# A spectral filter and a mixture of experts: experts' rows gathered without drains, three of them behind scatters, and a filter tile with its halves swapped

## The chip, the cores and the metric

The kernel runs on one core of one Trainium2 chip. The time is the device time of one execution in microseconds (us). A core has five engines, each with an instruction order of its own: PE (matrix products; its weight loads are shown as PEld), DVE (VectorE), ACT (ScalarE), POOL (GpSimd) and SP (SyncE, which issues transfers here). ACT and POOL issue transfers too. A transfer stands in the order of the engine that issues it, and an instruction that waits holds up all that stands behind it on that engine.

## The reference

Eight sequences of 2496 tokens with 256 channels are filtered in the frequency domain. The filtered tokens go to one of 8 experts each; an expert keeps the 80 tokens with the highest gate weight, and all other rows of the output are zero.

```python
X = np.fft.rfft(x, axis=1)                       # x: (8, 2496, 256)
y = np.fft.irfft(X * (filt_r + 1j * filt_i), n=2496, axis=1).reshape(19968, 256)
logits = y @ w_gate                              # 8 experts
expert_idx = np.argmax(logits, axis=1)
gate_w = softmax(logits)[arange, expert_idx]
for e in range(8):
    tok = the (at most) 80 tokens of expert e with the highest gate_w
    out[tok] = gate_w[tok, None] * (np.maximum(y[tok] @ w1[e], 0) @ w2[e])
```

`w1[e]` is 256 x 1024 and `w2[e]` 1024 x 256, all in float32.

## The kernel before

**Filtering.** The transform is done as matrix products with tables. `x` comes in chunks (`load_x`, tiles `x`), three for each of the 8 sequences. `stage1` multiplies a chunk with the table `wf_t`, `turn_t` transposes, `stage2` multiplies with the table `d_t` (tile `pb`), and `filtered` multiplies with the filter `ft` on DVE and adds on POOL (`yt`). The filter is brought into the order of `ft` at the start: `filter_in` loads five pieces (groups of four frequency rows) of `filt_r` from SP's queue and of `filt_i` from POOL's into the tile `fst`, whose partitions hold the real rows at places 0 and 1 of each four and the imaginary ones at 2 and 3; `filter_turn` multiplies `fst` with the permutation table `perm` into `pf`. On SP, each piece is followed by a piece of `d_t`, and behind the five pieces the x chunks 3 to 6. Ahead of the first piece stands a one-element copy on POOL from x chunk 1 into `fst[0, 0, 0]`. The tile framework sees that the loads into the real rows overwrite that element and lets them wait for the copy; so SP's filter loads, and all that stands behind them on SP, start when x chunk 1 has arrived. POOL's loads of the imaginary rows stand behind the copy in POOL's order.

**Gates and choice.** The filtered spectrum gives the gates directly (`gates`, `logits`, `gating`), and DVE finds the chosen tokens: `gating(3, 8)` turns the keys of the last two sequences on PE (`pk`), ACT copies them (`kt`), DVE takes the best eight of each row, `threshold` spreads them (`spread`), PE sums them up (`pall`), and DVE finds the threshold.

**Rows of the chosen tokens.** Only chosen tokens are transformed back. `gather_rows` fetches rows of a table with an indirect transfer on POOL (`gt`), `turn_rows` transposes them on DVE (`wt`), and `fill(n)` issues the next n of 20 products per tile that add up the tokens' rows (`pr`) from spectra kept in DRAM (`page`). There are seven such tiles; at the end of each, ACT copies it (`yr`) and writes it to `y_sel` in DRAM from its own queue. `fill` calls are set by hand between other work, and this fixes PE's order.

**Experts.** `experts(..., True)` runs the 8 experts. The rows of experts 0 and 1 are fetched ahead (`xg_first`) without the last tile, which a product adds. For experts 2 to 7, `gather(e)` fetches 80 rows of `y_sel` into a buffer `xg` on POOL, each followed by `nc.gpsimd.drain()`, by which POOL waits for what it has issued. In the loop, `layer1(e + 1)` (tile `ph`), `back(e - 1)` (tile `pb`, then `put`) and `layer2(e)` (tile `po`, with the turn `px` of the rows of expert e + 2 in its middle) follow each other on PE. `put` scales the result on ACT into one of two buffers `ys` and scatters it to the output with an indirect transfer on POOL. Each scatter writes the whole output tensor as far as the framework can see, so each waits for the one before to land; and `ys` of expert e waits for the scatter of expert e - 2. In POOL's order all six gathers stand ahead of the first scatter.

**Weights.** An expert's weights are one tile of two halves, `w1[e]` and `w2[e]`, loaded from SP (1 MB each, about). Tiles are reused, so a load waits for the last reader of the tile's former content. A `mark` is a one-element POOL memset into the tile ahead of the load: the load waits for it, and so for POOL to come to that place. `load_weights(3, ...)` is marked behind the gathers of experts 0 and 1, `load(4, ...)` behind the gather of expert 3. `load(5)` to `load(7)` follow in the loop.

`experts(..., False)` belongs to a branch for inputs that the fast path cannot hold; it is not taken here.

## Time and profile before

| what | value |
|---|---|
| three runs | 392.21, 395.75, 397.69 us; median 395.75 |
| the profiled execution, its own time | 397.52 us |
| its span, from the first to the last instruction | 395.7 us |
| mean granted PE clock | 0.969 |

The page gives, for each engine, busy time, share of the span and instructions; then the span in 40 slices of 9.9 us. A digit is a busy share in tenths; PEclk is the granted clock of PE in tenths of full speed.

```profile
PE 361.6 (91%) x4037; PEld 321.6 (81%) x4037; DVE 235.8 (60%) x509; ACT 131.1 (33%) x273; POOL 177.6 (45%) x256
...
PE   8789999999999999999999998999998998790793
...
POOL 3664355545646454444468887135534011201221
PEclk9999999999999999999999999999999999877597
...
GB/s 213 233 333 256 160 336 265 305 332 308 338 303 291 349 311 309 347 295 304 353 278 303 243 252 272 404 378 410 409 410 352 228 240 22 288 368 232 27 28 24
```

PE is busy in nearly every slice but the first and the last six. Those last slices hold the experts, from about 322 us on; there the clock drops as well. The transfers that the change touches are these (line, what goes where, issuing queue, count, size of each):

```profile
w<-in_moe_w_dram SPq DMA_DIRECT2D x16, 1024.0 KB
x<-in_x_dram SPq DMA_DIRECT2D x15, 936.0 KB
x<-in_x_dram SPq DMA_DIRECT2D x7, 702.0 KB
fst<-in_filt_i_dram POOLq DMA_DIRECT2D x10, 128.0 KB
fst<-in_filt_r_dram SPq DMA_DIRECT2D x10, 128.0 KB
```

### The profile page before, as it was taken

To read this page: it belongs to the slowest core of one execution; us is meant where nothing else is said; L and a number is where in the kernel's file an instruction comes from. 1 tells how busy PE (TensorE), PEld (TensorE's weight loads), DVE (VectorE), ACT (ScalarE), POOL (GpSimd) and SP (SyncE) were. 2 spreads that over 40 slices of the span, in tenths; PEclk is the share of its full clock that TensorE was granted. 3 is DMA by queue.
4 is the path that set the end of the run, shared out by engine and by line. 5 is a ranking of instruction groups with operands and counts; after the bars stand their busy time and mean duration, and the time that the engine had idled before them with its cause. 6 is when DMAs were issued, how large, how long until landed. Compare 5 with 4: busy or idle time off the path is not lost. (4 is left out here: it accounts for less than half of the span.)

```text
span 395.7 us, 9875 instructions
## 1 busy us (share of the span) xinstructions
PE 361.6 (91%) x4037; PEld 321.6 (81%) x4037; DVE 235.8 (60%) x509; ACT 131.1 (33%) x273; POOL 177.6 (45%) x256
## 2 busy tenths in 40 slices
PE   8789999999999999999999998999998998790793
PEld 7789989989899899799699896788864677690682
DVE  5037466748868668789797678899678311110010
ACT  2444545454455354444344452250000001000110
POOL 3664355545646454444468887135534011201221
PEclk9999999999999999999999999999999999877597
DMA  6798699999999999999988787999999670896000
GB/s 213 233 333 256 160 336 265 305 332 308 338 303 291 349 311 309 347 295 304 353 278 303 243 252 272 404 378 410 409 410 352 228 240 22 288 368 232 27 28 24
DMA packets 40975, 109.87 MB, mean 278 GB/s; under 512 B 3975, under 2 KB 14085, under 8 KB 39167
## 3 DMA queue, kind: packets, MB, share of 16 engines
q1 hardware_dynamic: 36008, 97.64, 72.8%
q0 software_dynamic: 3632, 10.46, 7.7%
q10 hardware_dynamic: 1282, 1.06, 0.8%
q8 instruction: 34, 0.56, 0.6%
q14 instruction: 19, 0.16, 0.1%
HBM read 70.35 MB, written 40.37 MB: 280 GB/s over the span
## 5 line engine op out<-in xcount | busy, mean ns | idle before, releaser
L356 POOL TENSOR_TENSOR yt<-p 128x256 f32<-128x256 f32 x159 | 114.9, 746 | 93.1 <-DVE p L348 90.3
L348 DVE TENSOR_TENSOR p<-pb,ft 128x1024 f32<-128x1024 f32 x80 | 97.3, 1217 | 55.7 <-PE pb L338 22.2
L313 PE MATMUL pa<-wf_t,x 117*128 117x120 f32 x704 | 92.0, 278 | 2.8 <-DMA x<-in_x_dram 2.8
L313 PEld LDWEIGHTS pa<-wf_t,x 117*128 117x128 f32 x704 | 86.2, 195 | 3.4 <-issue 2.9
L338 PE MATMUL pb<-d_t,t 128*128 128x128 f32 x640 | 84.9, 276 | 1.3 <-DVE p L348 1.2
L338 PEld LDWEIGHTS pb<-d_t,t 128*128 128x128 f32 x640 | 77.8, 192 | 2.0 <-ACT zt_last L422 1.2
L318 ACT COPY tt<-pa 128x480 f32<-128x480 f32 x96 | 47.9, 516 | 71.8 <-PE pa L313 70.7
L331 ACT COPY t<-pt 128x512 f32<-128x512 f32 x80 | 47.0, 588 | 18.4 <-PE pt L327 15.1
L369 DVE STREAM_TRANSPOSE u<-yt 128x512 f32<-128x512 f32 x70 | 48.9, 699 | 0.0
L327 PE MATMUL pt<-ident,tt 128*128 128x128 f32 x320 | 48.5, 274 | 0.5 <-ACT tt L318 0.5
L875 POOL DMA_INDIRECT gt<-rows_tbl,idxr x28 | 28.5, 1019 | 37.8 <-DVE wt L885 31.1
L327 PEld LDWEIGHTS pt<-ident,tt 128*128 128x128 f32 x320 | 37.4, 142 | 1.8 <-issue 1.6
L894 PE MATMUL pr<-page,wt 128*128 128x256 f32 x160 | 36.6, 382 | 0.1
L894 PEld LDWEIGHTS pr<-page,wt 128*128 128x128 f32 x160 | 29.6, 190 | 4.5 <-issue 0.9
L899 PE MATMUL pr<-page,wt 128*32 128x256 f32 x480 | 28.7, 380 | 1.1 <-issue 0.8
L885 DVE STREAM_TRANSPOSE wt<-gt 128x640 f32<-128x640 f32 x28 | 22.8, 830 | 7.3 <-DMA gt<-rows_tbl,idxr 7.0
L899 PEld LDWEIGHTS pr<-page,wt 128*32 128x32 f32 x480 | 15.6, 110 | 12.7 <-issue 2.0
L1215 DVE COPY xs_True<-px_True 128x160 f32<-128x160 f32 x8 | 2.6, 325 | 36.5 <-PE px_True L1212 24.7
L1196 POOL DMA_INDIRECT xg_True<-y_sel,idxg x6 | 5.7, 946 | 35.7 <-issue 35.7
L1245 PE MATMUL po_True<-hT_True,w 128*64 128x80 f32 x448 | 21.5, 258 | 0.0
L903 ACT COPY yr<-pr 128x256 f32<-128x256 f32 x7 | 2.6, 372 | 57.1 <-PE pr L894 27.0
L1227 PE MATMUL ph_True<-xs_True,w 128*64 128x80 f32 x512 | 20.9, 245 | 0.0
(215 smaller groups left out, 327.9 us busy)
## 6 DMA issues: line engine op xcount, KB each, us to landing
out_dram<-zero_t SPq DMA_DIRECT2D x32, 624.0 KB
yf<-u SPq DMA_DIRECT2D x56, 320.0 KB
page<-yf SPq DMA_DIRECT2D x14, 1280.0 KB
w<-in_moe_w_dram SPq DMA_DIRECT2D x16, 1024.0 KB
x<-in_x_dram SPq DMA_DIRECT2D x15, 936.0 KB
x<-in_x_dram SPq DMA_DIRECT2D x7, 702.0 KB
fst<-in_filt_i_dram POOLq DMA_DIRECT2D x10, 128.0 KB
fst<-in_filt_r_dram SPq DMA_DIRECT2D x10, 128.0 KB
```

Of the source, the lines that this page charges most:

```text
L313: nc.tensor.matmul(out=ps[:, j, :], rhs=wf_t, start=True, stop=True, lhsT=xt[3 * b + ch][:, j0 + j - JC * ch, 128 * cb:128 * cb + 128])
L318: nc.scalar.copy(out=tt[h][:, :, H3 * j0:H3 * j0 + hn * jn].rearrange("p s (j h) -> p s j h", h=hn), in_=v)
L327: nc.tensor.transpose(ps[:, i, :], tt[h][:, 2 * s:2 * s + 2, :].rearrange("p r n -> p (r n)"), ident[:])
L331: nc.scalar.copy(out=t2[k][:], in_=ps[:])
L338: nc.tensor.matmul(out=ps[:, :, i, :], lhsT=t[:, i, :], rhs=d_t[:, SG * g + i, :], start=True, stop=True)
L348: nc.vector.tensor_tensor(out=p[:], in1=f.unsqueeze(2).to_broadcast(shape), op=AL.mult, in0=ps[:].rearrange("p r s q -> p r (s q)").unsque ...
L356: eng.tensor_tensor(out=y[:, :, 2 * r:2 * r + 2, :], in0=a, in1=b, op=op)
L369: nc.vector.transpose(uu[h][:, :, SG * g:SG * g + SG, :].rearrange("p a s w -> p s a w"), spectrum(h)[:, SG * g:SG * g + SG])
L875: nc.gpsimd.indirect_dma_start(out=gts[t, g][:].rearrange("p s q -> p (s q)"), out_offset=None, in_=quarters, in_offset=bass.IndirectOffse ...
L885: nc.vector.transpose(wts[t][:, :, 32 * g:32 * g + 32], gts.pop((t, g))[:])
L894: nc.tensor.matmul(st["po"][:], lhsT=wts[t][:, s, :], rhs=columns(pages[t], s), **kw)
L899: nc.tensor.matmul(st["po"][at], lhsT=wts[t][:, s, at], rhs=columns(pages[source(t, g)[0]], s), **kw)
```

## The change

It has four parts.

1. The imaginary filter goes to places 0 and 1 of each four partitions of `fst` and the real one to 2 and 3; the table `perm` is swapped in the same way, so `ft` holds what it held. The one-element copy now touches the imaginary rows, which POOL loads; SP's loads of the real rows do not wait for it.
2. The four fills that stood behind `gating(3, 8)` stand ahead of it.
3. A drain is put on POOL behind the gathers of table rows for the last tile (`gather_all(6)`).
4. Experts: the gathers of 2, 3 and 4 stand in a row without drains. The gathers of 5, 6 and 7 move into the loop, each behind the scatter of expert 0, 1 and 2; one drain stands behind the last. The weights of expert 3 are loaded in two parts: `w1` where both were, `w2` with a mark of its own behind the gather of expert 3. The mark of expert 4's weights moves behind the gather of expert 4. There are four `xg` buffers instead of six, and three `ys` buffers instead of two.

```diff
-            perm.transpose(2, 0, 1, 3, 4).reshape(128, 2 * (NQ + NS - 1)).astype(f32))
+            perm[::-1].transpose(2, 0, 1, 3, 4).reshape(128, 2 * (NQ + NS - 1)).astype(f32))
...
-                        out=fst[2 * v + part:128:4, SG * g:SG * g + SG, :],
+                        out=fst[2 * (1 - v) + part:128:4, SG * g:SG * g + SG, :],
...
-        def load_weights(e, mark=None):
+        def load_first(e, mark=None):
             where, tag = WT[e]
             ws[e] = where.tile([128, NDB * FF + NFC * C], F32, name=f"w_{e}", tag=tag)
             if mark is not None:
                 mark(ws[e][:, 0:1], 0.0)
             nc.sync.dma_start(out=ws[e][:, 0:NDB * FF].rearrange("p (k f) -> p k f", k=NDB),
                               in_=moe_w1[e].rearrange("(k p) f -> p k f", p=128))
+
+        def load_second(e, mark=None):
+            if mark is not None:
+                mark(ws[e][:, NDB * FF:NDB * FF + 1], 0.0)
             nc.sync.dma_start(out=ws[e][:, NDB * FF:].rearrange("p (k d) -> p k d", k=NFC),
                               in_=moe_w2[e].rearrange("(k p) d -> p k d", p=128))
+
+        def load_weights(e, mark=None):
+            load_first(e, mark)
+            load_second(e)
...
-        fill(9)
+        fill(13)
         gating(3, 8)
-        fill(4)
...
         gather_all(6)
+        nc.gpsimd.drain()
...
-        load_weights(3, nc.gpsimd.memset)
+        load_first(3, nc.gpsimd.memset)
...
-            xg = fp.tile([cap, C], F32, name=f"xg_{first}_{e}", tag="xg", bufs=E - near)
+            xg = fp.tile([cap, C], F32, name=f"xg_{first}_{e}", tag="xg",
+                         bufs=4 if first else E)
...
-            ys = fp.tile([cap, C], F32, name=f"ys_{first}_{e}", tag="ys")
+            ys = fp.tile([cap, C], F32, name=f"ys_{first}_{e}", tag="ys", bufs=3)
...
-        for e in range(near, E):
+        for e in range(near, 5 if first else E):
             gather(e)
-            if first:
-                nc.gpsimd.drain()
             if first and e == 3:
+                load_second(3, nc.gpsimd.memset)
+            elif first and e == 4:
                 load(4, nc.gpsimd.memset)
...
             if e > 0:
                 back(e - 1)
+            if first and 0 < e < 4:
+                gather(e + 4)
+                if e == 3:
+                    nc.gpsimd.drain()
             layer2(e, (lambda: turn(e + 2)) if e + 2 < E else None)
```

POOL's order in the expert stage, before (drains are not listed; `w_3786` is the weight tile of expert 3, `w_3897` that of expert 4; `xg` are the gathers, `out_dram` the scatters):

```order
L1081 MEMSET w_3786 128x1
L1196 DMA xg_True_3887<-y_sel,idxg 80x256
L1196 DMA xg_True_3892<-y_sel,idxg 80x256
L1081 MEMSET w_3897 128x1
L1196 DMA xg_True_3901<-y_sel,idxg 80x256
L1196 DMA xg_True_3906<-y_sel,idxg 80x256
L1196 DMA xg_True_3911<-y_sel,idxg 80x256
L1196 DMA xg_True_3916<-y_sel,idxg 80x256
L1271 DMA out_dram<-ys_True_4092,idxs 19968x256
L1271 DMA out_dram<-ys_True_4180,idxs 19968x256
L1271 DMA out_dram<-ys_True_4268,idxs 19968x256
```

And the same stretch of POOL after the change (`w_3787` is expert 3's tile, `w_3901` expert 4's):

```order
L1081 MEMSET w_3787 128x1
L1205 DMA xg_True_3887<-y_sel,idxg 80x256
L1205 DMA xg_True_3891<-y_sel,idxg 80x256
L1087 MEMSET w_3787 128x1
L1205 DMA xg_True_3897<-y_sel,idxg 80x256
L1081 MEMSET w_3901 128x1
L1280 DMA out_dram<-ys_True_4076,idxs 19968x256
L1205 DMA xg_True_4081<-y_sel,idxg 80x256
L1280 DMA out_dram<-ys_True_4168,idxs 19968x256
L1205 DMA xg_True_4173<-y_sel,idxg 80x256
L1280 DMA out_dram<-ys_True_4260,idxs 19968x256
L1205 DMA xg_True_4265<-y_sel,idxg 80x256
```

The first scatter has moved ahead of the last three gathers, expert 4's mark behind one gather more, and a second mark of expert 3's tile stands between the gathers of experts 3 and 4.

On PE, at the turn of the last keys (`pk`), the difference is this (`pr` are the fills of the first tile, `pq` the turn of the last page):

```order
-L894 MATMUL pr_2959<-page_2401,wt_2721 128x256 x9
-L506 MATMUL pk_3058<-ident,key 128x128 x3
-L894 MATMUL pr_2959<-page_2401,wt_2721 128x256 x4
+L894 MATMUL pr_2959<-page_2401,wt_2721 128x256 x13
+L506 MATMUL pk_3065<-ident,key 128x128 x3
 L383 MATMUL pq_3107<-ident,yt 128x128 x4
```

The four fills are the last of their tile, so on ACT, in the same place, the copy of the tile (`yr`) and its write move as well:

```order
-L509 COPY kt<-pk_3058 128x3x128
-L903 COPY yr_3067<-pr_2959 128x256
-L904 DMA y_sel<-yr_3067 128x256
+L903 COPY yr_3062<-pr_2959 128x256
+L904 DMA y_sel<-yr_3062 128x256
+L509 COPY kt<-pk_3065 128x3x128
 L385 COPY page_3073<-pq_3107 128x4x4x32
```

The copy of the turned keys (`kt`) now stands behind both.

## The prediction

> **What bounds the kernel now.** I read the waits of the matmul engine (PE) first, because PE is busy for 361.6 of the 395.7 us: only its idle time and its slow clock can be won. The rows name the waiting instruction, the work that ended the wait, the total, the count and the longest.
>
> ```profile
> PE pb_True L1263 <- ACT ys_True L1269: 12.1, 1, 12.1
> PE px_True L1212 <- DMA xg_True<-y_sel,idxg: 4.1, 2, 2.7
> PE pf L534 <- DMA fst<-in_filt_r_dram: 1.2, 3, 0.7
> PE pk L506 <- DVE key L501: 0.7, 1, 0.7
> PE pall L568 <- DVE n L563: 0.5, 1, 0.5
> ```
>
> Sixteen of these 18.6 us lie in the expert stage. One wait of 12.1 us is the largest thing in the kernel. To see what stands behind it, I read the timeline of POOL, ACT and the DMA queues from 298 us on (start, length, engine, work, idle time before it).
>
> ```profile
> 298.78 1.01 POOL L875 DMA_INDIRECT gt<-rows_tbl,idxr  x1 [6.74 <-DVE wt L885]
> ...
> 302.71 1.00 POOL L875 DMA_INDIRECT gt<-rows_tbl,idxr  x1 [0.30 <-DVE tk_h L1391]
> 313.14 0.33 ACTq L904 DMA_DIRECT2D y_sel<-yr  x1
> 315.64 0.97 POOL L1178 DMA_INDIRECT xg_first<-y_sel,idxg  x1 [11.93 <-DMA y_sel<-yr]
> 321.78 0.33 ACTq L904 DMA_DIRECT2D y_sel<-yr  x1
> 328.15 0.95 POOL L1196 DMA_INDIRECT xg_True<-y_sel,idxg  x1 [10.16 <-issue]
> 333.63 0.95 POOL L1196 DMA_INDIRECT xg_True<-y_sel,idxg  x1 [4.54 <-issue]
> 335.08 0.47 ACT L1269 ACTIVATE ys_True<-pb_True,gate 80x256 f32<-80x256 f32 x1 [1.11 <-PE pb_True L1263]
> 336.79 0.10 POOL L1081 MEMSET w<- 128x1 f32 x1 [2.21 <-PE px_True L1212]
> 337.52 0.95 POOL L1196 DMA_INDIRECT xg_True<-y_sel,idxg  x1 [0.64 <-issue]
> 345.15 0.95 POOL L1196 DMA_INDIRECT xg_True<-y_sel,idxg  x1 [6.69 <-issue]
> 360.73 0.94 POOL L1196 DMA_INDIRECT xg_True<-y_sel,idxg  x1 [6.77 <-issue]
> 365.59 0.96 POOL L1271 DMA_INDIRECT out_dram<-ys_True,idxs  x1 [3.91 <-SPq L1378]
> 368.03 0.47 ACT L1269 ACTIVATE ys_True<-pb_True,gate 80x256 f32<-80x256 f32 x1 [18.15 <-DMA out_dram<-ys_True,idxs]
> 368.73 0.93 POOL L1271 DMA_INDIRECT out_dram<-ys_True,idxs  x1 [2.18 <-ACT ys_True L1269]
> 390.17 0.91 POOL L1271 DMA_INDIRECT out_dram<-ys_True,idxs  x1 [2.16 <-ACTq L1378]
> ```
>
> The result of expert 0 (`ys`) stands ready at 335.6 us, but its scatter leaves at 365.59: in POOL's order it stands behind six gathers, each with a drain. `ys` has two buffers, so the third result waits for that scatter to land (18.15 us on ACT), and PE waits for ACT. The drains show as idle POOL time: 4.54 us behind the first gather, 6.69 and 6.77 us behind gathers beside the loads of weights. Four gathers without drains (298.78 to 302.71) leave 1.31 us apart.
>
> Now PE in the same stage. `px` is the turn of an expert's gathered rows, `ph` its first layer, so from `ph` to `ph` is one expert's step.
>
> ```profile
> 330.71 0.36 PE L1212 MATMUL px_True<-ident,xg_True 80*128 80x80 f32 x2 [1.44 <-DMA xg_True<-y_sel,idxg]
> 332.16 2.38 PE L1227 MATMUL ph_True<-xs_True,w 128*64 128x80 f32 x64
> ...
> 336.23 0.20 PEld L1212 LDWEIGHTS px_True<-ident,xg_True 80*128 80x128 f32 x2 [0.24 <-DMA xg_True<-y_sel,idxg]
> ...
> 337.67 2.38 PE L1227 MATMUL ph_True<-xs_True,w 128*64 128x80 f32 x64
> ...
> 344.35 0.53 PE L1212 MATMUL px_True<-ident,xg_True 80*128 80x80 f32 x2 [2.69 <-DMA xg_True<-y_sel,idxg]
> ...
> 347.00 4.12 PE L1227 MATMUL ph_True<-xs_True,w 128*64 128x80 f32 x64
> ...
> 379.66 2.43 PE L1227 MATMUL ph_True<-xs_True,w 128*64 128x80 f32 x64
> ...
> 385.55 3.62 PE L1256 MATMUL po_True<-w,hT_True 128*80 128x256 f32 x16
> ```
>
> A step without a stall takes 5.51 us (332.16 to 337.67). Windows show the clock beside the waits; the columns after the busy times are granted clock, DMA share and GB/s.
>
> ```profile
> 344.00:346.00 2.00, 1.65 (x20) 1.48 (x22) 0.33 (x1) 0.00 (x0) 0.85 (x1) 0.50 1.08 393
> ...
> 350.00:352.00 2.00, 2.00 (x42) 1.72 (x40) 0.49 (x1) 0.00 (x0) 0.00 (x0) 0.85 1.03 356
> ...
> 362.00:364.00 2.00, 0.00 (x0) 0.00 (x0) 0.00 (x0) 0.00 (x0) 0.00 (x0) 0.50 0.31 97
> ```
>
> After the wait of 2.69 us the clock stands at 0.50 until about 350 us: the stall costs again behind itself. The loads run until about 362.5 us.
>
> **The change part by part.** *Gathers and scatters.* Six drains leave the gathers' path, and one comes back behind the last gather. The second half of expert 3's weights goes behind gather 3, so only 1 MB instead of 2 MB is in flight when the last tile is written to `y_sel` at 321.78. The nearest row for such a write with few loads beside it is the one issued at 313.14, whose reader starts at 315.64, 2.50 us later. So gather 2 leaves at 321.78 + 2.50 = 324.3 instead of 328.15. Gathers 3 and 4 follow at 1.31 us, plus about 0.7 us for a mark, and the loads of expert 4 start near 328.7 instead of 336.9, behind the moved half: 9 MB at the present pace (8 MB in some 24.5 us, 338 to 362.5) end near 356. The last two pieces are needed by PE at 358 and 364, so the loads stay hidden, by a margin of a few us.
>
> PE then runs at its own pace: the 1.44 us at 330.71 go, and the five steps from 332.16 to 379.66 take 5 x 5.51 = 27.55 instead of 47.50 us. That is 1.44 + 19.95 = 21.4 us, the half clock included.
>
> What is late next is POOL's chain, for scatters wait for each other: 368.73 follows 365.59 by 3.14 us though its `ys` was long ready. How long a scatter takes beside loads no row shows. Below stands the 2.2 us between the end of one scatter's row and the start of the next (366.55 to 368.73), without loads; above 6.8 us, the idle time behind a drained gather beside loads. The nearest is a gather beside loads whose reader is seen: 338.47 to 344.35, 5.9 us. I take 5.9. Then `ys` 0 is ready at 334.1 (1.44 earlier), scatter 0 leaves at 334.4, gather 5 at 335.7; scatter 1 leaves at 341.5 and gather 6 at 342.7, landing at 349.6, needed at 351.3 (`px` comes 4.07 us into a step, 332.16 to 336.23); scatter 2 leaves at 348.6 and gather 7 at 349.8, landing at 356.7, needed at 356.8. Just in time. The drain behind it ends near 357.4; there scatter 3 leaves, and 4 to 7 follow at 3.1 us, the last at 369.8. PE alone would have it at 390.17 - 21.4 = 368.8, so the chain takes back 1.0: **-20.4 us**. Three `ys` buffers are enough here: `ys` 3 needs scatter 0, landed at 341.2.
>
> [...]
>
> The drain behind the last row gathers (302.71) costs nothing: POOL's next work waits until 315.64 for the `y_sel` write. Four `xg` buffers: gathers 6 and 7 take those of 2 and 3, read by `px` 12 us before.
>
> *Thirteen fills before `pk`.* Four fills (matmuls of the row products) move ahead of the turn of the keys.
>
> ```profile
> 250.47 4.05 PE L894 MATMUL pr<-page,wt 128*128 128x256 f32 x18
> 255.22 0.52 PE L506 MATMUL pk<-ident,key 128*128 128x128 f32 x3 [0.70 <-DVE key L501]
> ...
> 255.78 0.87 ACT L509 COPY kt<-pk 128x384 f32<-128x384 f32 x1 [3.06 <-PE pk L506]
> ...
> 259.46 0.42 DVE L558 TENSOR_TENSOR spread<-row,thot 128x256 f32<-128x256 f32 x1
> ...
> 259.94 0.70 PE L568 MATMUL pall<-spread,same_f 128*128 128x256 f32 x2
> ```
>
> A fill is 4.05 / 9 = 0.45 us, so 13 end at 250.47 + 5.85 = 256.3, where `pk` starts 1.1 us later than now, without its 0.70 us wait. But `pk` begins a chain (ACT's copy, then VectorE to `spread`) for which `pall` already waits 0.5 us. PE does the same work ahead of `pall` in either order, so `pall` moves by what `pk` moves: +1.1, and up to +1.5 where ACT first copies `yr` and issues its write. The other end is -0.7, if nothing hung on `pk`. The `pall` wait is the nearest row: **+1.3 us**.
>
> *The filter halves.* SP's loads of the real filter, and the `d_t` tables and x loads behind them, no longer wait for x chunk 1.
>
> ```profile
> 12.87 5.14 PE L313 MATMUL pa<-wf_t,x 117*128 117x120 f32 x44 [1.72 <-DMA x<-in_x_dram]
> ...
> 11.00:12.00 1.00, 0.15 (x2) 0.00 (x0) 0.00 (x0) 0.56 (x1) 0.00 (x0) 1.00 0.81 223
> 12.00:13.00 1.00, 0.13 (x1) 0.16 (x2) 0.00 (x0) 0.00 (x0) 0.21 (x2) 1.00 0.43 141
> ```
>
> The gain ends at the 1.2 us that PE waits at `pf`. The risk is chunk 1, for which PE idles until 12.87, when the first three chunks (2.6 MB) have all but arrived: chunk 2, behind it in the queue, was moved with it. Some 1 MB of filter and `d_t` now follows chunk 2; if it shared as freely, at 250 GB/s chunk 1 would be 3.9 us later, +2.7 net. With chunk 2 between them I take 0.5 us of delay, **-0.7 us**. [...]
>
> **Sum.** -20.4 + 1.3 - 0.7 = -19.8 us, so the span goes from 395.7 to 375.9. The profiled execution took 397.52, of which 1.8 lies around the span; it is the slower end of the three runs (392.21 to 397.69). On their median of 395.75 the same loss gives 376.0.
>
> **The rivals.** *POOL's chain binds harder.* At the bound of 6.8 us gather 7 lands 1.7 us late and the chain ends 1.8 us later: 377.8. At 8 us, beyond any row (scatters and gathers then crowd one queue), gather 6 lands at 353.9, PE waits 2.6 us at `px`, and the clock halves as behind the 2.69 us wait, about 2.9 us more (the step from 337.67 to 347.00 has 3.82 above 5.51, of which 2.69 is the wait, and the `ph` at 347.00 another 1.74). PE's own end moves to 368.8 + 5.5, the part is -15.9, and the time 380.5. For it: gather 7's margin is 0.1 us. Against it: the loads thin out by then. [...]
>
> *All parts fall well.* Transfers beside loads land in 2.2 us, `pk` gains 0.7, the filter gains 1.2, and the 0.24 us that PE's weight load (PEld) at 336.23 waits inside the 5.51 us step goes five times: -21.4 - 1.9 - 1.2 gives 371.3. [...]
>
> *Chunk 1 is late* by the full 3.9 us: 376.0 + 3.4 = 379.4.
>
> *The idle POOL time belongs to the transfer, not to the drain*, and the change does not do what it says. Each gather would hold POOL some 7.6 us beside loads (337.52 to 345.15), and scatters, which no row shows beside loads, perhaps 9. Then gathers 3 and 4 leave near 329.8 and 334, scatter 0 at 342, gather 5 at 351, scatter 1 at 359, gather 6 at 368 (the loads are through), scatter 2 at 371 and gather 7 at 374, landing at 377. From there PE takes 12.0 us to the last scatter (356.8 to 368.8 above) and 2.9 for the half clock: 391.9 instead of 390.17, and with the other parts 398.1, slower than now. With 7.6 us for scatters too it is 395.3; it turns slower from about 8 us on. Against it stand the four gathers 1.31 us apart at 298.78 to 302.71.
>
> **How the numbers follow.** Forecast as summed: 0.68. POOL's chain harder: 0.13. All parts well: 0.08. Chunk 1 late: 0.04. Gathers hold POOL: 0.07, of which 0.02 ends slower and 0.05 within 2% (holds a little shorter). About 2% (7.9 us) is what a measurement of this kernel tells from no change. So faster 0.93, same 0.05, slower 0.02. The range, 371.3 to 381, holds the first four cases; its ends come from the two rivals' bounds.
>
> **What would show it.** In the changed profile: gathers 2 to 4 within 4 us of each other from 324 to 325 on; the 12.1 us wait at `pb` gone and the clock at 1.00 through the experts; each `px` wait under 1.5 us; scatters 0 to 2 some 7 us apart, later ones 3.1 us; the wait at `pk` gone and that at `pall` near 1.5 to 2 us; no waits at `pf`, and PE's work on chunk 1 still starting near 13. Wrong it would be if POOL shows idle stretches of 5 us behind undrained gathers, if PE waits over 3 us for `xg` or for weights, or if chunk 1 starts after 15 us.

## The result, and the profile after

The changed kernel was measured four times, each time beside the kernel before on the same chip.

| measurement | changed, median (lowest to highest) | before, median | ratio, 95% interval |
|---|---|---|---|
| first | 383.0 us (380.5 to 384.0) | 396.7 us | 0.968 [0.958, 0.979] |
| second (e4) | 384.8 us (379.2 to 386.9) | 397.2 us | 0.963 [0.955, 0.971] |
| third (e9) | 379.1 us (376.6 to 382.4) | 397.7 us | 0.952 [0.947, 0.957] |
| fourth (e15) | 382.2 us (379.3 to 386.8) | 398.3 us | 0.956 [0.951, 0.961] |

An execution is called disturbed here when it took over 1.5% longer than the fastest of its kernel in the same measurement: the medians hold such executions, the ratios leave them out, and the profiles of e1, e11, e14 and e15 are of such executions.

It is faster, by 12 to 19 us. The prediction had 376.0 us, 371.3 to 381.0, from 395.75: the direction is right, the gain of 19.8 us is too large, and the first measurement lies above the range.

First the waits of PE in the profile after (total, count, longest).

```profile
PE pa L313 <- DMA x<-in_x_dram: 4.5, 4, 2.5
PE pall L568 <- DVE n L563: 2.2, 2, 1.7
PE po_True L1254 <- issue: 1.7, 2, 0.9
PE misc L833 <- DVE vsum L830: 1.6, 1, 1.6
PE ph_True L1236 <- issue: 0.8, 1, 0.8
```

The 12.1 us at `pb`, the 4.1 us at `px` and the 1.2 us at `pf` are gone. What stands there instead is small and spread: x, the wait at `pall` that was forecast, and two kinds that were not: `misc`, and "issue", where PE waits for nothing that these rows name.

The timeline of POOL in the expert stage (start, length, engine, work, idle time before it), with the last write of `y_sel` ahead of it:

```profile
326.86 0.33 ACTq L904 DMA_DIRECT2D y_sel<-yr  x1
...
329.42 0.94 POOL L1205 DMA_INDIRECT xg_True<-y_sel,idxg  x1 [6.36 <-PE px_True L1218]
...
331.92 0.95 POOL L1205 DMA_INDIRECT xg_True<-y_sel,idxg  x1 [0.19 <-issue]
...
339.25 0.96 POOL L1280 DMA_INDIRECT out_dram<-ys_True,idxs  x1 [6.27 <-ACT ys_True L1278]
...
346.12 0.95 POOL L1280 DMA_INDIRECT out_dram<-ys_True,idxs  x1 [4.63 <-DMA out_dram<-ys_True,idxs]
...
352.66 0.93 POOL L1280 DMA_INDIRECT out_dram<-ys_True,idxs  x1 [4.32 <-issue]
353.90 0.97 POOL L1205 DMA_INDIRECT xg_True<-y_sel,idxg  x1 [0.30 <-issue]
...
369.69 0.91 POOL L1280 DMA_INDIRECT out_dram<-ys_True,idxs  x1 [3.92 <-ACT ys_True L1278]
...
376.61 0.91 POOL L1280 DMA_INDIRECT out_dram<-ys_True,idxs  x1 [2.22 <-ACTq L1391]
```

Gathers 2 to 4 leave within 2.5 us of each other. Scatter 0 leaves right behind its result at 339.25, and scatters 1 and 2 follow 6.9 and 6.5 us apart. Scatter 3 leaves only at 361.71, when the drain behind the gather at 353.90 is through; the prediction had 357.4. From scatter 5 on (369.69) POOL waits for ACT's results, that is for PE: the chain of scatters no longer sets the end.

PE in the same stage, from the second `ph` on:

```profile
335.73 2.38 PE L1236 MATMUL ph_True<-xs_True,w 128*64 128x80 f32 x64
...
341.09 2.81 PE L1236 MATMUL ph_True<-xs_True,w 128*64 128x80 f32 x64
...
346.88 0.23 PE L1236 MATMUL ph_True<-xs_True,w 128*64 128x80 f32 x1
...
347.89 2.43 PE L1236 MATMUL ph_True<-xs_True,w 128*64 128x80 f32 x63 [0.78 <-issue]
...
354.13 0.36 PE L1254 MATMUL po_True<-hT_True,w 128*64 128x80 f32 x4 [0.79 <-issue]
...
354.26 2.44 PE L1236 MATMUL ph_True<-xs_True,w 128*64 128x80 f32 x64
...
360.47 0.51 PE L1254 MATMUL po_True<-hT_True,w 128*64 128x80 f32 x9 [0.90 <-issue]
...
366.17 2.38 PE L1236 MATMUL ph_True<-xs_True,w 128*64 128x80 f32 x64
```

No `px` waits any more, but PE stops in the middle of a product: behind one matmul of 64 at 346.88, behind 28 of 32 ahead of 354.13. From the first gap to the second and from the second to the third lie 127 matmuls. The five steps take 30.44 us (335.73 to 366.17).

The next table cuts the span at the starts of six groups on PE and at the last scatter. e9 is the changed kernel once more, e10 a version explained below.

| stretch | before | after | difference | predicted | e9 | e10 |
|---|---|---|---|---|---|---|
| start to the first `pz` | 52.5 | 49.8 | -2.7 | -0.7 | 52.9 | 49.5 |
| first `pz` to the first `pz_last` | 186.6 | 192.5 | +5.9 | 0 | 186.6 | 186.0 |
| to the `pall` behind `pk` | 20.8 | 22.1 | +1.3 | +1.3 | 22.1 | 22.1 |
| to `pe_s` | 37.9 | 37.4 | -0.5 | 0 | 37.2 | 37.1 |
| to the first `px` | 23.4 | 24.6 | +1.2 | 0 | 22.9 | 22.0 |
| to the last scatter | 69.0 | 50.3 | -18.6 | -20.4 | 50.6 | 50.1 |
| to the end | 5.5 | 5.6 | +0.1 | 0 | 5.6 | 5.9 |
| span | 395.7 | 382.2 | -13.5 | -19.8 | 377.8 | 372.8 |

So the experts fell 1.8 us short, and the rest of the miss lies in stretches that the change does not touch or only touches from afar: 5.9 us from the first `pz` to `pz_last`, 1.2 us ahead of the first `px`. In the first of them, the row of PE's wait and two windows (granted clock, DMA share and GB/s stand last):

```profile
128.73 2.89 PE L313 MATMUL pa<-wf_t,x 117*128 117x120 f32 x12 [2.50 <-DMA x<-in_x_dram]
```

```profile
128.00:130.00 2.00, 1.27 (x6) 1.30 (x7) 0.17 (x1) 0.00 (x0) 0.01 (x1) 0.67 0.92 261
130.00:132.00 2.00, 2.00 (x11) 2.00 (x11) 0.00 (x0) 0.85 (x2) 0.00 (x0) 0.50 1.00 339
```

An x chunk is 2.5 us late, and the clock stands at 0.50 behind that. The second place is the wait at `misc`, and the clock in windows behind it:

```profile
308.14 0.16 PE L833 MATMUL misc<-vsum,ones_bf 128*128 128x1 bf16 x1 [1.58 <-DVE vsum L830]
```

```profile
309.00:311.00 2.00, 2.00 (x28) 1.10 (x32) 1.09 (x3) 0.00 (x0) 0.00 (x0) 0.65 1.03 400
311.00:313.00 2.00, 2.00 (x24) 0.94 (x20) 0.84 (x1) 0.00 (x0) 0.00 (x0) 0.50 1.03 382
```

A wait of 1.58 us is followed by a stretch at half clock. The experiments ask which of these belong to the change.

### The profile page after: what moved, and what is told of

It reads as the page before. It is cut to its first block, busy times and chain, and to the rows that moved or that the text cites. A ratio compares the mean times of both kernels' runs of the same rounds, so it can differ in the third digit from the quotient of the medians.

```text
span 382.2 us, 9877 instructions
## 1 busy us (share of the span) xinstructions
PE 358.7 (94%) x4037; PEld 319.9 (84%) x4037; DVE 235.6 (62%) x509; ACT 131.2 (34%) x273; POOL 177.3 (46%) x257
## 5 line engine op out<-in xcount | busy, mean ns | idle before, releaser
L348 DVE TENSOR_TENSOR p<-pb,ft 128x1024 f32<-128x1024 f32 x80 | 97.4, 1217 | 58.5 <-PE pb L338 27.3
L313 PE MATMUL pa<-wf_t,x 117*128 117x120 f32 x704 | 93.6, 281 | 5.6 <-DMA x<-in_x_dram 4.5
L313 PEld LDWEIGHTS pa<-wf_t,x 117*128 117x128 f32 x704 | 87.4, 198 | 6.7 <-issue 3.6
L327 PEld LDWEIGHTS pt<-ident,tt 128*128 128x128 f32 x320 | 37.4, 142 | 1.8 <-issue 1.6
L899 PEld LDWEIGHTS pr<-page,wt 128*32 128x32 f32 x480 | 17.0, 114 | 10.9 <-issue 2.0
L1280 POOL DMA_INDIRECT out_dram<-ys_True,idxs x8 | 7.4, 931 | 33.3 <-ACT ys_True L1278 15.3
L1236 PE MATMUL ph_True<-xs_True,w 128*64 128x80 f32 x512 | 19.6, 233 | 0.9 <-issue 0.8
L1254 PE MATMUL po_True<-hT_True,w 128*64 128x80 f32 x448 | 18.8, 236 | 1.7 <-issue 1.7
L1236 PEld LDWEIGHTS ph_True<-xs_True,w 128*64 128x64 f32 x512 | 18.5, 137 | 1.3 <-issue 1.2
```

The lines of the kernel that those rows point to most:

```text
L313: nc.tensor.matmul(out=ps[:, j, :], rhs=wf_t, start=True, stop=True, lhsT=xt[3 * b + ch][:, j0 + j - JC * ch, 128 * cb:128 * cb + 128])
L327: nc.tensor.transpose(ps[:, i, :], tt[h][:, 2 * s:2 * s + 2, :].rearrange("p r n -> p (r n)"), ident[:])
L348: nc.vector.tensor_tensor(out=p[:], in1=f.unsqueeze(2).to_broadcast(shape), op=AL.mult, in0=ps[:].rearrange("p r s q -> p r (s q)").unsque ...
L899: nc.tensor.matmul(st["po"][at], lhsT=wts[t][:, s, at], rhs=columns(pages[source(t, g)[0]], s), **kw)
L1236: nc.tensor.matmul(ph[c:c + 64, i, 0:cap], lhsT=w1[:, k, f:f + 64], rhs=xs[:, k, :], start=(k == 0), stop=(k == NDB - 1))
```

## The experiments

**e1, e2, e3, e4: the parts apart, and the changed kernel again.** e1 undoes the swap of the filter halves:

```diff
-            perm[::-1].transpose(2, 0, 1, 3, 4).reshape(128, 2 * (NQ + NS - 1)).astype(f32))
+            perm.transpose(2, 0, 1, 3, 4).reshape(128, 2 * (NQ + NS - 1)).astype(f32))
...
-                        out=fst[2 * (1 - v) + part:128:4, SG * g:SG * g + SG, :],
+                        out=fst[2 * v + part:128:4, SG * g:SG * g + SG, :],
```

> The changed kernel with the filter halves as they were before (parts 2 to 4 of the change alone). The changed kernel took 383.0 us and its profile shows the start 2.0 us ahead until 97 us, then x late at 128.7 us by 2.5 us, with the clock at 0.59 behind it, so that PE stands 3.2 us behind at 168 us: 5.2 us lost in the middle. Theory A (the earlier start is what makes x late, since x comes by a queue that is nearly full): without the swap the stall at 128 us is gone and the time is about 383.0 - 3.2 = 379.8 us. Theory B (the late x is chance of one execution; the swap is worth its 2 us): 385.0 us. Theory C (the middle is bound by the transfers, so that 2 us gained at the start are lost again wherever they stand): 383 us, within 0.7 us.

e2 is the same two lines the other way round, put alone into the kernel before.

> The kernel before with the filter halves swapped and nothing else. The kernel before took 396.7 us. Theory A (the earlier start makes x late): 3 us slower, about 399.9 us, with a wait for x of over 2 us near 128 us in the profile. Theory B (chance): 2 to 2.7 us faster, about 394.4 us. Theory C (the middle is bound by transfers): 396.7 us, within 0.7 us; the waits at the filter's turn are gone in each case.

e3 is the kernel before with all lines of the fourth part, and none of the other three.

> The kernel before with the fourth part alone: gathers 2 to 4 in a row without drains, 5 to 7 behind scatters, expert 3's second half of weights and expert 4's weights marked later, three result buffers; neither swap nor fills nor the drain behind the last row gathers. The prediction had 20.4 us for it, so 376.3 us from 396.7. The profile pair shows 18.6 us from the first turn of an expert's rows on (321.21 to 395.7 before, 326.29 to 382.2 after): 378.1 us. If the late x and the half clock at 309 us of the changed kernel are its own chance, this kernel shows 378 us; if the drain behind the last row gathers or the fills cost more than predicted, this kernel stands further below the changed one than 5 us.

> The changed kernel once more, for a second profile. If the wait for x near 128 us (2.5 us and a half clock behind it) and the half clock behind the wait at 308 us belong to the change, both are here again and the time is 383 us; if they were chance, at least one is missing in this profile, and the time of this execution is 3 to 5 us lower.

e1 took 380.9 us (0.960 [0.955, 0.964]), e2 397.7 us (1.002 [0.998, 1.007]), e3 379.6 us (0.954 [0.948, 0.961]), e4 384.8 us. e2 speaks against A (399.9) and B (394.4): the swap alone moves nothing that can be measured. e1 lies nearest to A, and its interval, some 4 us wide, reaches to C (383). In e2's profile the late x stands at the start and not at 128 us; in e4's the stretch from `pz` to `pz_last` takes 188.1 us instead of 192.5. The 2.5 us wait at 128 us was thus one execution's, while waits for x somewhere are in all profiles. The half clock behind `misc` was there again in e4, and not in e2, with the same wait of 1.57 us. e3 shows that the fourth part alone brings 17.6 us of the forecast 20.4 (medians).

**e5: the loads of the late weights taken away.** Experts 5 to 7 compute with the weights of experts 2 to 4:

```diff
             if n < E:
-                load(n)
+                if first:
+                    ws[n] = ws[n - 3]
+                else:
+                    load(n)
```

> The changed kernel without the weight loads of experts 5 to 7; these use the weights that stand in the tiles of experts 2 to 4, so 6 MB less move beside the experts' products. In three profiles of the new expert stage PE stands still in the middle of a product, 0.8 to 1.45 us at a time, 127 matmuls apart, with nothing that the profile shows as its reason. Theory A (what PE waits for there is brought by a transfer that stands behind the weights): with few loads the gaps are gone, the five steps take 5 x 5.36 = 26.8 us instead of 30.4, and the time is about 3.5 us below the changed kernel. Theory B (the gaps belong to the place in the program): they stay at 0.8 us each, and the time is that of the changed kernel within 1 us. Under A scatters also follow each other at about 3.1 us instead of 6.5 to 6.9.

It took 377.8 us (0.949 [0.943, 0.955]). The rows of `ph` on PE:

```profile
333.47 2.38 PE L1236 MATMUL ph_True<-xs_True,w 128*64 128x80 f32 x64
...
338.83 2.86 PE L1236 MATMUL ph_True<-xs_True,w 128*64 128x80 f32 x64
...
344.68 2.38 PE L1236 MATMUL ph_True<-xs_True,w 128*64 128x80 f32 x64
...
360.77 2.38 PE L1236 MATMUL ph_True<-xs_True,w 128*64 128x80 f32 x64
```

The gaps are gone from 344 us on, where the loads end (25 to 38 GB/s in windows from 342 us on, where the changed kernel has 363 to 393), and one of 0.5 us is left at 338.83, beside the last loads. Five steps take 27.30 us instead of 30.44. Theory A holds: what PE waits for comes late because of the weights' traffic. What that is, the packed trace tells, which lists every packet of a transfer. The queue q8, marked "instruction", has packets of 16,384 bytes. In the profile after, those of 345.21 to 346.38, 351.48 to 352.52 and 357.91 to 359.00 us end 1.5, 1.6 and 1.5 us before PE goes on at 347.89, 354.13 and 360.47. They start 3.6 to 3.8 us after PE has passed the place 256 instructions ahead of the stop; in e5, without the loads, the packets for the same places start 0.3 to 1.5 us after it and take nearly as long (0.9 to 1.0 us, against 1.0 to 1.2). So each stop ends behind such a packet, which starts late beside the weights; what a packet holds the trace does not show.

The scatters then leave 5.0 to 6.2 us apart instead of 6.5 to 6.9, now because they wait for PE; how close they could follow is not seen, so the 3.1 us expected there stays unproven. That stage accounts for 3.1 us of the 5 to 7 us below the changed kernel's first two measurements. The rest is not split up: this profile has no half clock behind `misc`, but it has one behind `pall`.

**e6 and e7: six fills moved ahead of `misc`.**

```diff
         load_weights(2)
-        fill(4)
+        fill(10)
         st["misc2"]()
         last_hot(0)
         last_hot(1)
-        fill(16)
+        fill(10)
```

> The changed kernel with six fills moved from behind the products misc and pd to ahead of them. In its two profiles PE waits 1.57 us there, and the clock stands at 0.50 for 3.4 us from 309 us on, so that the next products take 17.4 instead of 15.75 us. Theory A (the wait brings the half clock): the wait is filled, the clock stays at 1.00, and the time falls by 1.57 + 1.7 = 3.3 us at most, to about 379.7 us. Theory B (the wait is a real limit, and PE only waits later, for the same chain): the time stays at 383 us within 1 us.

> The experts' part alone (e3) with the same six fills moved ahead of misc and pd. e3 measured 379.6 us; its profile has a wait of 0.97 us there and no half clock. Theory A: 378 us, 1 to 1.6 us below e3, and up to 3.3 where the clock would have been halved. Theory B: 379.6 us. It keeps the filter halves of before, so its start shows once more when x chunk 1 is there: near 11 us, where the three profiles with the swap had 12.0, 14.2 and 15.4.

e6 took 377.9 us (0.950 [0.945, 0.956]), e7 382.7 us (0.962 [0.958, 0.967]). The wait at `misc` is gone in both profiles, and from `pe_s` to the first `px` it takes 22.6 and 22.1 us, where the changed kernel has 24.6 with the half clock and 22.9 without. Theory A holds for the place. The totals don't follow it: e7 is 3.1 us above e3, and its profile shows why: 190.0 us from `pz` to `pz_last`, where e3's has 186.0. (The 15.4 in e7's expectation was misread; x chunk 1 was begun at 12.5 there. In e7, without the swap, it was 13.7.)

**e8: the kernel before without its six drains.**

```diff
             gather(e)
-            if first:
-                nc.gpsimd.drain()
```

> The kernel before without the six drains behind the experts' gathers, and nothing else: the order with all gathers ahead of the first scatter, two result buffers and the old marks stay. Theory A (the drains alone kept the gathers apart and the first scatter late): gathers 4 to 7 leave 1.3 us apart, scatter 0 leaves right behind its result near 336 us, the wait of 12 us at pb is gone, and the time is 397 - 15.5 = 381.5 us; only the first 1.44 us at px and what the scatters take back remain. Theory B (gathers beside loads hold POOL whether drained or not, and the order decides): scatter 0 leaves past 350 us, and the time is above 390 us.

It took 390.4 us (0.981 [0.975, 0.987]). Neither theory has that. The last scatter, and the span:

```profile
378.85 0.91 POOL L1271 DMA_INDIRECT out_dram<-ys_True,idxs  x1 [2.35 <-ACTq L1376]
```

```profile
span 389.5 us, 9869 instructions
```

A is right about the stage: scatter 0 leaves 0.7 us behind POOL's last gather (339.47), the wait of 12 us is gone, and from the first `px` to the last scatter it takes 53.8 us instead of 69.0, 15.1 less, as A had (15.5). So the drains are most of the 18.6 us of the change; with the new order and marks the same stretch takes 50.1 to 52.1 us in the undisturbed profiles of the changed kernel, e3, e6, e7, e10 and e12, 1.8 to 3.7 us less than here. But the program ends 10.65 us after the last scatter, where it was 5.5 us. Five microseconds came back at the end.

**e9 to e12, beside each other on one chip:** the changed kernel (e9), e6 again (e10), e10 with the filter halves as before (e11), and e10 without any drain (e12):

```diff
         gather_all(6)
-        nc.gpsimd.drain()
...
                 gather(e + 4)
-                if e == 3:
-                    nc.gpsimd.drain()
```

> The changed kernel once more, beside e10 to e12 on the same chip, to measure the moved fills of e6 and the swap within one call. So far it took 383.0 and 384.8 us. If the half clock behind the 1.57 us wait at misc (here twice in two profiles, but missing in e2, e5 and e8 with the same wait) depends on where the wait falls in the clock's own windows, it may be missing here; if it belongs to the change, it is here a third time.

> e6 again: the changed kernel with six fills ahead of misc and pd. By theory A of e6 it is 1.6 to 3.3 us below e9 (the wait, and the half clock where it comes), so some 380 us; e6 measured 377.9, 5 us below the changed kernel, of which up to 2 us would then be chance of the x loads. Without effect (theory B) it equals e9 within 1 us.

> e10 with the filter halves as before. In five profiles each, the first spectra (pz) start at 51.6 us on average with the swap (48.6 to 53.6) and at 52.0 without it (49.4 to 53.2). Theory A (the swap is worth nothing that can be seen, since what it saves at the filter's turn is smaller than the spread of x's arrival): equal to e10 within 1.5 us. Theory B (it costs, since x chunk 1 shares with the filter): 2 to 3 us faster than e10. Theory C (it is worth its 1.2 us and more): 1.2 to 2 us slower.

> e10 without the two drains that the change keeps on POOL (behind the row gathers of the last tile, and behind the gather of expert 7). In e8, without any drain behind experts' gathers, the program ended 10.65 us after its last scatter (378.85 to 389.5), where all other profiles have 5.5 to 5.6 us. Theory A (a drain only postponed comes back at the end, where it is waited for): the tail is 10.6 us again and the time 4 to 5 us above e10. Theory B (the longer tail of e8 was chance): the tail is 5.6 us, and the time that of e10 within 1 us.

e9 took 379.1 us (0.952), e10 378.3 us (0.951 [0.946, 0.956]), e11 379.5 us (0.952 [0.947, 0.956]), e12 384.5 us (0.964 [0.959, 0.969]).

e9 has the wait of 1.57 us at `misc` and no half clock. A window behind that wait:

```profile
308.00:310.00 2.00, 2.00 (x44) 1.23 (x40) 0.85 (x1) 0.00 (x0) 0.00 (x0) 1.00 1.04 398
```

In the six undisturbed profiles with this wait (the first of the changed kernel, e2, e4, e5, e8, e9) the half clock came in two. The packed traces list when the clock changed: in each profile all its changes lie on a grid of 3.413 us. The two waits with the half clock begin 0.4 us behind and 0.1 us ahead of a point of this grid, the four without it 1.8 to 2.4 us behind one. So the place on the grid separates them, and it differs between executions of one kernel (e4 and e9). The grid is what the traces show of the clock's windows in the expectations of e9 and e14. e10 is 0.8 us below e9, half of the 1.6 us expected at least; in its profile 22.0 us stand from `pe_s` to `px` against 22.9. The intervals overlap, so the timing alone shows no gain. e11 equals e10 within the 1.5 us of theory A: the swap is worth nothing that can be measured, nor does it cost.

e12 settles e8. The last scatter and the span of e12, and then the last scatter of e10, whose span is 372.8 us:

```profile
372.16 0.91 POOL L1279 DMA_INDIRECT out_dram<-ys_True,idxs  x1 [3.13 <-DMA out_dram<-ys_True,idxs]
```

```profile
span 382.7 us, 9875 instructions
```

```profile
366.86 0.91 POOL L1280 DMA_INDIRECT out_dram<-ys_True,idxs  x1 [2.23 <-ACTq L1391]
```

The tail is 10.54 us without drains and 5.94 with them. The median is 6.2 us longer (5.4 by the ratios), near the 4 to 5 of theory A. Where the tail grows is seen in POOL's own drains on the program's last line (shortest, median and longest in ns, then the first and last start), in e12 and then in e10:

```profile
L1783 POOLq DRAIN  x3: 46/103/4807, 377.0 to 382.4; - x3
```

```profile
L1786 POOLq DRAIN  x3: 46/103/452, 371.3 to 372.5; - x3
```

Each of these programs ends with such drains. The longest takes 4.8 us in e12 and e8, and 0.45 us in e10 and the changed kernel. e3 and e7 have the drain behind the last gather alone, and their tails are 5.5 us: that one drain is enough. What a drain does in this time no run shows.

**e13 to e15, another chip:** the changed kernel without the zero rows (e13), with a longer wait at `misc` (e14), and as it is (e15).

```diff
     def put_zeros(n, todo=None):
-        todo = zeros if todo is None else todo
+        if todo is None:
+            del zeros[:n]
+            return
```

> The changed kernel without the 20 MB of zero rows that it writes to the output between 43 and 200 us, so that x, yf and pages move alone there. In fourteen profiles PE waits between 0.8 and 7.2 us for x, the later part of it at places that change from one execution to the next, and the stretch from the first spectra (pz) to the last (pz_last) takes 186 to 194 us in kernels that are the same there. Theory A (the crowded transfers make x late by chance, and this is most of what lies between the 383 to 385 us of two measurements and the 379 us of a third): all waits for x after 20 us are gone, the stretch takes 186 us or less, and the time is 375 to 379 us, with less spread. Theory B (the stretch is bound by the engines, and the spread comes from elsewhere): the stretch and the time stay as in e15.

```diff
         load_weights(2)
-        fill(4)
         st["misc2"]()
         last_hot(0)
         last_hot(1)
-        fill(16)
+        fill(20)
```

> The changed kernel with the four fills that stand right ahead of misc moved behind pd, so that the wait there grows from 1.57 to about 2.6 us. Theory A (half clock from idle time in one of the clock's windows, by chance of position for 1.57 us, always for longer waits): the clock is at 0.50 behind it, and from the product pe_s to the first turn of expert rows (px) it takes 24.6 us, as in the three profiles with the half clock, plus up to 1 us. Theory B (the half clock has nothing to do with this wait): 22.9 us plus 1 us at most, clock 1.00.

> The changed kernel beside e13 and e14 on the same chip: 379 to 385 us as before, its waits for x after 20 us between 0 and 3 us and, with the wait of 1.57 us at misc, the half clock or not.

e13 took 379.6 us (378.6 to 383.2), e15 382.2 us (379.3 to 386.8). In e13's profile all waits for x but the two at the start are gone, and the stretch from `pz` to `pz_last` takes 186.0 us:

```profile
PE pa L315 <- DMA x<-in_x_dram: 3.3, 2, 1.8
```

That is what theory A says of the waits, but it is one profile, and e3, e10 and e12 have the zero rows, no wait for x behind 20 us and the same 186.0 us. The time lies 0.6 us above the range of A, its interval overlaps that of e15, and the spread of 4.6 us against 7.5 rests on six executions each. So crowding by the zero rows is likely and not shown. What remains on this chip stands in the experts: 52.9 us from `px` to the last scatter in e13, against 50.1 to 50.7 in five profiles (the first, e4, e6, e9, e10): 7.2 us lie between its second and third `ph`, where the others have 4.9, with four gaps of 0.3 us whose cause the profile does not show.

e14 took 388.4 us. Its wait grew more than meant, because four fills take 2.1 us there and not 1:

```profile
309.92 0.16 PE L833 MATMUL misc<-vsum,ones_bf 128*128 128x1 bf16 x1 [3.76 <-issue]
```

It has the half clock (0.50 from 309.0 to 315.8 us, two steps of the grid) and 27.3 us from `pe_s` to `px`, where A had at most 25.6. Of the excess of 1.7 us, 1.2 us is the wait itself, 3.76 against 2.6. So a longer wait does bring the half clock here, as A said; one profile, of a disturbed execution, does not show that it always does. The other three executions of e14 have a mean clock of 0.979 to 0.988, the undisturbed ones of e15 0.991 to 0.997, which fits.

## Why the prediction was wrong, point by point

**Experts, -20.4 us: right in its mechanism, 2 us too large.** The failed step is "PE then runs at its own pace": five steps at 5.51 us, 27.55 us. They took 30.44 us, since PE now runs beside the loads of weights, where it stops once in 127 matmuls (0.78, 0.79 and 0.90 us). e5 without the late loads has none of these stops from 344 us on, and 27.30 us. The 5.51 us came from the step at 332 us, where next to no transfers ran; the steps behind it hold the waits of 2.69 and 12.1 us, and no such stop shows there. The step's window in the profile before, and the stage in the profile after (GB/s stand last):

```profile
332.00:337.00 5.00, 4.92 (x124) 4.39 (x122) 1.14 (x3) 0.91 (x2) 1.04 (x2) 1.00 0.06 20
```

```profile
340.00:360.00 20.00, 17.92 (x420) 15.96 (x420) 3.74 (x10) 2.72 (x6) 5.01 (x6) 1.00 1.06 370
```

On the other side, the 1.0 us that POOL's chain was to take back did not come: scatters landed 6.5 to 6.9 us apart where 7.1 was assumed, and behind the loads the results of PE come last. The two errors, 2.9 and 1.0 us, partly cancel by luck. Net: 18.6 us instead of 20.4.

The smaller steps hold. Gather 2 left 2.56 us behind the write of `y_sel` (2.50 predicted), gathers 3 and 4 followed at 1.25 us (1.31), as all six of e8 do, so the rival in which a gather holds POOL without a drain is refuted. No `px` waited (gather 7 at 353.90, read at 364.73), the loads of weights stayed hidden, three `ys` buffers were enough, and four `xg` buffers too. The clock is at 1.00 through the stage. Only the later scatters did not follow at 3.1 us: they came 3.1 to 4.9 us apart, behind 9.1 us for the drain. The list of transfers of the profile after gives the gathers' median from issue to landing:

```profile
xg_True<-y_sel,idxg POOLq DMA_INDIRECT x6, 5.7
```

5.9 us was taken for it.

**Drains: a price that the sum lacked, though it did no harm here.** The prediction costed drains by what they delay, and the last one at little. It did not ask what they are worth. e8 and e12 show it: without any, the end is 4.6 to 5.1 us later, mostly because the drain at the program's end takes 4.8 us instead of 0.45. The change keeps one, and so lost nothing.

**Fills ahead of `pk`, +1.3 us: confirmed for the stretch to `pall`, with a price behind it that the sum lacked.** The wait at `pk` is gone, `pall` waits 1.67 us, and the stretch to `pall` is 1.3 us longer in the first profile, in e4, e6, e9 and e10, and unchanged in e2 and e3, which lack this part:

```profile
259.43 0.37 ACT L903 COPY yr<-pr 128x256 f32<-128x256 f32 x1 [3.57 <-PE pr L894]
...
260.21 0.87 ACT L509 COPY kt<-pk 128x384 f32<-128x384 f32 x1 [0.40 <-PE pq L383]
```

In the profile after (start, length, engine, work), ACT turns to the keys (`kt`) behind the copy of the tile and its write, as the order showed. The next stretch, to `pe_s`, gives some of it back: 37.1 to 37.4 us in the undisturbed profiles with this part but e5, 37.7 to 38.4 in those without. And the longer wait at `pall`, 1.67 us where it was 0.5, has a half clock behind it in some profiles. A window of e5 behind that wait:

```profile
263.00:266.00 3.00, 3.00 (x15) 2.92 (x14) 2.76 (x14) 1.28 (x3) 2.02 (x2) 0.50 1.03 418
```

It happened in e5 and in the disturbed profiles of e11, e14 and e15, four of twelve with this part and none of five without it, and the stretch to `pe_s` takes 38.5 to 39.4 us there. In these four the wait begins 1.4 to 1.7 us behind a point of the clock's grid, in the other eight 0.4 to 0.9 or 2.2 to 3.0 us behind one.

**Filter halves, -0.7 us: neither confirmed nor refuted.** The waits at `pf` are gone in all profiles with the swap, as said. But x chunk 1 is begun between 10.1 and 14.2 us from one execution to the next, with the swap (10.9 to 14.2) as without (10.1 to 13.7). The first `pz` stands at 51.5 us on average in nine profiles with the swap (48.6 to 53.6) and at 52.6 in four without (51.8 to 53.2): 1.2 us, near the 0.7 predicted, in a spread of 5; with the disturbed profiles the averages are 51.4 and 52.0. e2 and e11 give no difference in time. The rival of a chunk 1 that is late by 3.9 us is refuted as an effect of the swap.

**The drain behind the row gathers, 0: confirmed.** POOL's next gather waits for `y_sel` in any case, 13.1 us (320.73), and leaves 2.5 us behind the write, as before.

**What no step of the sum held: 7 us in the profile pair.** This is the larger part of the first measurement's miss: the sum put the stretches that the change does not touch at nothing, without a term for how far they differ from one execution to the next. 5.9 us of it lie between `pz` and `pz_last`: 3.0 us are two waits for x, 1.7 the half clock behind the longer one, and 1.1 a wait that the rows put down to ACT (at 98 us). This stretch takes 185.99 to 192.5 us over the undisturbed profiles, changed or not. That crowded transfers make x late fits e13 and is not shown; why one execution hits it and the next does not is open. The other 1.2 us is the half clock behind `misc` (1.7 us, less 0.5 us ahead of it), present in the first profile and in e4, absent in e9. Against these 7 us stand 2.0 us at the start and 0.5 us ahead of `pe_s`, which came out better than the sum. The late x and the half clock come and go with the execution. They are the larger differences between the profiles of the first two measurements and that of e9; that they also set the medians apart is likely and not shown. The prediction's range, 371.3 to 381, was built from the change's own unknowns and left out the 5.5 us by which three runs of the kernel before already differed.

By the trace alone the change is worth -18.6 + 1.3 and about -0.7, some 18 us, which the third measurement shows (-18.6). It lies in the predicted range in part by luck: its profiled execution had no wait for x above 0.4 us behind 20 us and no half clock behind `misc`. The other three gains are 2 to 6 us smaller, and the share of each cause in them was not settled.

**A version that is as fast or faster.** e10 and e6 (the changed kernel with six fills ahead of `misc`) measured 0.951 and 0.950 of the kernel before, below all four measurements of the changed kernel. Against e9, measured beside e10, the difference is 0.8 us, within the intervals; what is shown is that the wait at `misc` and the half clock behind it are gone.

## What to carry to other kernels

When a long stall is removed, the work behind it can run beside other traffic than before: take its pace from a stretch with that traffic, not from the one clean step (here 30.44 us against 27.55). Before a drain or a wait is deleted, ask what will do its work later: here five microseconds came back at the end of the program, where no wait of PE points to them. And where runs of the same kernel already differ by more than the terms in dispute, the range has to hold that spread as well, and a second profile of the same kernel tells more than a finer reading of the first.

## What the runs showed of the hardware

**Beside the loads of weights (363 to 393 GB/s) PE stopped every 127 matmuls in the changed kernel.** Each stop is 0.4 to 1.5 us; without the loads (25 to 38 GB/s, e5) it is gone. With one weight load for each matmul, 127 matmuls are 254 instructions; with the few of PE's instructions that do not count as busy, the packed trace has 256 from each stop to the next, at the same places of PE's order in all profiles of the changed kernel. The profile lists a queue of its own for instructions:

```profile
q8 instruction: 34, 0.56, 0.6%
```

34 packets with 0.56 MB are 16,384 bytes each. PE has 8206 instructions in the packed trace of the profile after, 32.1 times 256. That one packet brings PE the 256 instructions from stop to stop is an estimate from these numbers; no run shows what a packet holds. In the profile after, a packet starts 3.6 to 3.8 us after PE has passed the place 256 instructions before, takes 1.0 to 1.2 us, and PE goes on 1.5 to 1.6 us after its end: 6.2 to 6.3 us for 256 instructions, which take PE 5.2 us in e5.

**Behind a wait of 1.6 us the clock was halved in some profiles, depending on its place.** Behind the wait at `misc` it was in two of six undisturbed profiles, for 3.4 us (the products behind took 17.4 instead of 15.75 us), behind the one of 1.67 us at `pall` in one of eight, and behind a wait of 3.8 us in e14. The clock changed only on a grid of 3.413 us, and the place on it told the waits with the half clock from those without. What makes the grid, no run shows.

**With the drains left out the end came later:** 10.5 to 10.65 us from the last scatter to the end (e8, e12), 5.3 to 5.9 us in all other profiles; POOL's drain at the program's end takes 4.81 us in these two and 0.45 to 0.71 us in the others.
